# Exp writes runs of 32 tokens, the token order is restored by a permutation matrix in the transpose of x, and all PSUM tiles share four two-bank slots

## Chip, cores, metric

One core of one Trainium2 chip. The metric is the device time of one execution in microseconds (us). In the profile, PE is the engine of matmuls, PEld its weight loads, ACT the scalar engine, DVE the vector engine, POOL the GpSimd engine that issues the casting loads, SP the engine that issues stores.

## The reference

Attention over keys and values that are averaged over 8 neighbouring tokens, then a gated feed-forward block with a convolution of width 3 along the tokens:

```python
# batch 8, heads 8, tokens 576, head dim 64; keys and values pooled to 72
scores = scale * q @ mean8(k).T;  attn = softmax(scores);  y = attn @ mean8(v)
x = y.transpose(0, 2, 1, 3).reshape(8, 576, 512)
h = relu(x @ w_in)                       # 512 -> 1024
c = conv_w[0]*h[t-1] + conv_w[1]*h[t] + conv_w[2]*h[t+1]
out = (h * sigmoid(c)) @ w_out           # 1024 -> 512
```

The queries are loaded with the tokens of a head spread over 96 partitions. The softmax division comes after the product with v, through a column of constants beside v.

## The kernel before

It works batch by batch. While the feed-forward of batch b runs in eight blocks `fb` (mm1, relu, conv, tanh, gate), the attention of batch b+1 is woven in; then mm2 writes the output. A scheduler orders the instructions of each engine at build time, from its own estimate; every engine then executes its list in that fixed order. Cuts are marked with `# ...`.

```python
big_psum = tile_pool(name="big_psum", bufs=3, PSUM)   # two banks each: scores, mm1, conv
one_psum = tile_pool(name="one_psum", bufs=2, PSUM)   # one bank each: all else
q_view = "h (p c) d -> p h c d"          # partition p holds tokens 6p .. 6p+5, 1536 bytes in a row
# ...
def scores(b, h):
    ps = big_psum.tile([P, 2, 512], FP32, name="sc_ps", tag="big")
    for c2 in range(2):                  # two matmuls: tokens of even and of odd c
        nc.tensor.matmul(out=ps[0:Sp, c2, 0:SC], lhsT=kz[b % 2][:, h, c2, :], rhs=qT[:, h % 2, :], ...)
    at = attnT_pool.tile([Sp, S], BF16, name="attnT")
    nc.scalar.activation(                # writes into token order: a step of 6 bf16 = 12 bytes
        out=at.rearrange("s (p cp c2) -> s c2 cp p", cp=QC // 2, c2=2),
        in_=ps[0:Sp, :, 0:SC].rearrange("s c2 (cp p) -> s c2 cp p", cp=QC // 2),
        func=ACT.Exp, scale=1.0 / (POOL * 8.0))
def av(b, i, g):                         # tile i of 128 tokens, four heads: one bank
    ps = one_psum.tile([P, 4, D + 1], FP32, name="av_ps", tag="one")
    # ... four matmuls, one reciprocal of 4 columns, one product into x (256 columns)
def xt(b, i):                            # four transposes of one token tile, one copy to xT
    ps = one_psum.tile([P, n_pairs, P], BF16, name="xt_ps", tag="one")
    # ...
def mm2(b, j):                           # one output tile: one bank, eight matmuls
    ps = one_psum.tile([P, d_model], FP32, name="o_ps", tag="one")
    # ...
```

The softmax here doesn't subtract the row's maximum and nothing guards it: scores larger than these inputs give would overflow.

## Time and profile before

357.72 us, median of two runs (357.71 and 357.73); the profiled execution spans 355.1 us.

| what | value |
|---|---|
| first feed-forward matmul starts at | 40.5 us |
| fifth and sixth batch together (198.5 to 279.0 us) | 80.5 us, 40.25 each |
| from the first to the last exp of such a batch | 18.7 us |
| ACT busy in a middle batch | 26.0 us, of that exps 16.1 |
| PE busy in a middle batch | 31.3 us |

A batch is counted here from its first mm1 matmul to that of the next. The page's line of busy times, with its share of the span, and the chain that ended last:

```profile
PE 264.0 (74%) x2049; PEld 169.0 (48%) x2049; DVE 176.3 (50%) x497; ACT 210.4 (59%) x209; POOL 26.4 (7%) x55
...
ACT 40%; PE 37%; DVE 14%; issue 5%; DMA 3%; ACTq 0%
ACT attnT L182 32%; PE o_ps L277 17%; PE h_ps L238 9%; PE c_ps L257 7%; ACT tg L265 4%; DVE x L206 4%; DMA v_126<-in_v_dram 3%; ACT hT L245 3%; PE av_ps L195 2%; DVE gT L271 2%; DVE o L288 2%; PE xt_ps L219 1%; DVE xT L221 1%; DVE r L205 1%; PE q_ps L152 1%
```

No engine is busy throughout, but a third of the span hangs on one line, the exp. The groups of instructions show why (line, engine, operation, output and input, count; then busy us, the mean of one in ns, idle time before them and what ended it):

```profile
L182 ACT ACTIVATE attnT<-sc_ps 72x576 bf16<-72x576 f32 x64 | 128.0, 2216 | 13.4 <-PE sc_ps L165 13.4
...
L245 ACT ACTIVATE hT<-h_ps 128x576 bf16<-128x576 f32 x64 | 48.1, 754 | 36.9 <-PE h_ps L238 36.9
L265 ACT ACTIVATE tg<-c_ps 128x576 bf16<-128x576 f32 x64 | 41.9, 654 | 8.4 <-PE c_ps L257 4.7 <-DVE tg_2126 L269 0.4 <-DVE tg_1219 L269 0.4
L206 DVE TENSOR_TENSOR x<-av_ps,r 128x256 bf16<-128x256 f32 x80 | 33.5, 419 | 0.8
```

Exp, relu and tanh each work on 576 columns. The exp takes 2.2 us where the others take 0.65 to 0.75. The table of stretches, two of one batch and two whole batches (stretch and its length, then busy time and count by engine, granted PE clock, DMA share, GB/s):

```profile
93.20:112.20 19.00, 11.63 (x95) 7.94 (x94) 6.17 (x16) 19.00 (x16) 0.79 (x1) 1.00 0.53 93
112.20:130.60 18.40, 16.74 (x131) 9.72 (x130) 11.87 (x36) 5.05 (x9) 0.17 (x2) 1.00 0.13 48
198.50:238.90 40.40, 31.46 (x264) 20.12 (x261) 18.15 (x55) 26.00 (x26) 0.94 (x3) 1.00 0.20 48
238.90:279.00 40.10, 31.23 (x255) 20.41 (x254) 16.37 (x52) 25.96 (x26) 0.17 (x2) 0.96 0.07 27
```

The first line is the exp stretch: ACT (the fifth number) is busy for all 19.00 us. In the second line PE (the second number) is busy for 16.74 of 18.40.

PE's waits on DVE, from the list of waits (us in total, times, longest):

```profile
PE av_ps L195 <- DVE x L206: 4.7, 8, 0.7
PE xt_ps L219 <- DVE x L206: 4.2, 9, 0.8
PE o_ps L277 <- DVE o L288: 4.1, 7, 0.7
```

### The profile page before, as it was taken

The numbers are of one execution on the slowest core, as the hardware profiler recorded it, in microseconds if no ns is written. First come the engines' busy times: TensorE is split into PE (matmuls) and PEld (weight loads), VectorE is DVE, ScalarE is ACT, GpSimd is POOL, SyncE is SP. The second block draws the span as 40 slices with busy tenths as digits, with TensorE's granted clock in tenths as the row PEclk, the third lists the DMA queues.
The fourth block names the chain that finished last, engine by engine and source line by source line (L and its number), as shares of the span: only waits on it lengthen the run. The fifth ranks groups of instructions, "written<-read, shape, count | busy, mean of one in ns | idle before, by whom it ended". The sixth has DMA issues, their size and how long they took to land.

```text
span 355.1 us, 5143 instructions
## 1 busy us (share of the span) xinstructions
PE 264.0 (74%) x2049; PEld 169.0 (48%) x2049; DVE 176.3 (50%) x497; ACT 210.4 (59%) x209; POOL 26.4 (7%) x55
## 2 busy tenths in 40 slices
PE   0163686789867896688777896689757898689995
PEld 0141464454545554464545554464635555454752
DVE  4672875696624934275425742283414732273341
ACT  1097049940798229960898139950996239960751
POOL 7250102112000000000000000000000000000000
PEclk9999999898999999899989999999998998999999
DMA  7999992969950030401140030501100030001103
GB/s 178 228 197 204 167 168 32 178 87 131 242 77 8 0 150 0 68 0 61 59 66 3 23 127 0 69 0 65 55 0 2 3 147 0 2 0 61 59 20 130
DMA packets 26957, 27.23 MB, mean 77 GB/s; under 512 B 3869, under 2 KB 21173, under 8 KB 26933
## 3 DMA queue, kind: packets, MB, share of 16 engines
q0 software_dynamic: 20464, 15.09, 30.0%
q1 hardware_dynamic: 5844, 10.63, 8.4%
q10 hardware_dynamic: 624, 1.18, 1.3%
q8 instruction: 16, 0.26, 0.3%
q14 instruction: 9, 0.07, 0.1%
HBM read 32.52 MB, written 9.44 MB: 118 GB/s over the span
## 4 chain that ended last, share of the span: by engine, by line
ACT 40%; PE 37%; DVE 14%; issue 5%; DMA 3%; ACTq 0%
ACT attnT L182 32%; PE o_ps L277 17%; PE h_ps L238 9%; PE c_ps L257 7%; ACT tg L265 4%; DVE x L206 4%; DMA v_126<-in_v_dram 3%; ACT hT L245 3%; PE av_ps L195 2%; DVE gT L271 2%; DVE o L288 2%; PE xt_ps L219 1%; DVE xT L221 1%; DVE r L205 1%; PE q_ps L152 1%
## 5 line engine op out<-in xcount | busy, mean ns | idle before, releaser
L182 ACT ACTIVATE attnT<-sc_ps 72x576 bf16<-72x576 f32 x64 | 128.0, 2216 | 13.4 <-PE sc_ps L165 13.4
L238 PE MATMUL h_ps<-xT,w_in_sb 128*128 128x288 bf16 x512 | 84.6, 304 | 2.0 <-DVE xT L221 0.5
L257 PE MATMUL c_ps<-hT,dw 128*128 128x288 bf16 x384 | 62.5, 295 | 20.3 <-ACT attnT L182 19.9
L245 ACT ACTIVATE hT<-h_ps 128x576 bf16<-128x576 f32 x64 | 48.1, 754 | 36.9 <-PE h_ps L238 36.9
L277 PE MATMUL o_ps<-w_out_sb,gT 128*128 128x512 bf16 x288 | 65.6, 382 | 5.7 <-DVE o L288 4.1
L238 PEld LDWEIGHTS <-w_in_sb 128*128 128x128 bf16 x512 | 49.6, 102 | 19.5 <-issue 5.9
L286 ACT COPY o<-o_ps 128x512 f32<-128x512 f32 x16 | 9.4, 586 | 77.9 <-PE o_ps L277 77.9
L257 PEld LDWEIGHTS <-dw 128*128 128x128 bf16 x384 | 37.6, 101 | 35.7 <-issue 25.5
L265 ACT ACTIVATE tg<-c_ps 128x576 bf16<-128x576 f32 x64 | 41.9, 654 | 8.4 <-PE c_ps L257 4.7
L277 PEld LDWEIGHTS <-gT 128*128 128x128 bf16 x288 | 27.6, 98 | 39.1 <-issue 6.0
L288 DVE COPY o<-o_ps 128x512 f32<-128x512 f32 x20 | 13.8, 691 | 44.2 <-PE o_ps L277 44.2
L206 DVE TENSOR_TENSOR x<-av_ps,r 128x256 bf16<-128x256 f32 x80 | 33.5, 419 | 0.8
L195 PEld LDWEIGHTS <-attnT 72*128 72x128 bf16 x320 | 18.8, 104 | 27.2 <-ACT attnT L182 13.4
L158 DVE COPY qT<-q_ps 128x576 bf16<-128x576 bf16 x32 | 14.6, 457 | 31.4 <-PE q_ps L152 31.0
L205 DVE RECIPROCAL r<-av_ps 128x4 f32<-128x4 f32 x80 | 13.8, 177 | 25.1 <-PE av_ps L195 24.4
L165 PE MATMUL sc_ps<-qT,kz_107 128*72 128x288 bf16 x64 | 14.3, 325 | 14.4 <-ACT attnT L182 8.5
L195 PE MATMUL av_ps<-va_109,attnT 72*128 72x65 bf16 x160 | 13.8, 208 | 11.8 <-ACT attnT L182 8.0
L165 PE MATMUL sc_ps<-qT,kz_108 128*72 128x288 bf16 x64 | 13.4, 304 | 10.6 <-ACT attnT L182 9.7
L219 PE MATMUL xt_ps<-ident,x 128*128 128x128 bf16 x160 | 18.0, 234 | 4.2 <-DVE x L206 4.2
L221 DVE COPY xT<-xt_ps 128x512 bf16<-128x512 bf16 (+1 forms) x40 | 15.7, 392 | 2.9 <-PE xt_ps L219 2.9
L219 PEld LDWEIGHTS <-x 128*128 128x128 bf16 x160 | 11.3, 102 | 11.5 <-DVE x L206 8.5
L195 PE MATMUL av_ps<-va_110,attnT 72*128 72x65 bf16 x160 | 12.1, 199 | 6.0 <-ACT attnT L182 3.1
(231 smaller groups left out, 186.8 us busy)
## 6 DMA issues: line engine op xcount, KB each, us to landing
out_dram<-o SPq DMA_DIRECT2D x36, 256.0 KB
kr<-in_k_dram POOLq DMA_DIRECT2D x7, 576.0 KB, 13.5
qr<-in_q_dram POOLq DMA_DIRECT2D x7, 576.0 KB, 6.4
vr<-in_v_dram POOLq DMA_DIRECT2D x7, 576.0 KB, 13.1
w_in_sb<-in_moe_w_in_dram POOLq DMA_DIRECT2D x4, 256.0 KB, 14.2
w_out_sb<-in_moe_w_out_dram POOLq DMA_DIRECT2D x2, 512.0 KB, 12.6
v_112<-in_v_dram ACTq DMA_DIRECT2D x2, 288.0 KB
k_111<-in_k_dram SPq DMA_DIRECT2D x2, 288.0 KB
```

Source lines behind the costliest of these rows:

```text
L165: nc.tensor.matmul(out=ps[0:Sp, c2, 0:SC], lhsT=kz[b % 2][:, h, c2, :], rhs=qT[:, h % 2, :], start=True, stop=True,)
L182: nc.scalar.activation(out=at.rearrange("s (p cp c2) -> s c2 cp p", cp=QC // 2, c2=2), in_=ps[0:Sp, :, 0:SC].rearrange("s c2 (cp p) -> s c ...
L195: nc.tensor.matmul(out=ps[:, hh, :], lhsT=st[b]["at"][h][:, t0:t0 + P], rhs=va[b % 2][:, h, :], start=True, stop=True,)
L206: nc.vector.tensor_tensor(out=st[b]["x"][i][:, 4 * g:4 * g + 4, :], in0=ps[:, :, 0:D], in1=r.unsqueeze(2).to_broadcast([P, 4, D]), op=OP.mult,
L219: nc.tensor.transpose(out=ps[:, pr, :], in_=x[:, 2 * pr:2 * pr + 2, :], identity=ident)
L221: nc.vector.tensor_copy(out=st[b]["xT"][:, :, i * P:tok0[i] + P], in_=ps[:, :, new:P])
L238: nc.tensor.matmul(out=ps[:, c, 0:SC], lhsT=w_in_sb[:, dc, fb * P:(fb + 1) * P], rhs=xT[:, dc, c * SC:(c + 1) * SC], start=(dc == 0), stop ...
L245: nc.scalar.activation(out=hT[:, fb, 1:S + 1].rearrange("p (c n) -> p c n", c=NS), in_=ps[:, :, 0:SC], func=ACT.Relu, scale=0.5,)
L257: nc.tensor.matmul(out=ps[:, c, 0:SC], lhsT=dw[:, fb, kk, :], rhs=hT[:, fb, c * SC + kk:c * SC + kk + SC], start=(kk == 0), stop=(kk == KW ...
L265: nc.scalar.activation(out=tg.rearrange("p (c n) -> p c n", c=NS), in_=ps[:, :, 0:SC], func=ACT.Tanh)
L277: nc.tensor.matmul(out=ps, lhsT=gT[:, fb, j * P:(j + 1) * P], rhs=w_out_sb[:, fb, :], start=(fb == 0), stop=(fb == n_fb - 1),)
L288: nc.vector.tensor_copy(out=o, in_=ps)
```

## The change

Its intent is to make the exp's writes nearly contiguous. q is loaded as pairs of neighbouring tokens, so that one score matmul makes the even tokens and the other the odd ones. The exp then writes runs of 32 even and 32 odd tokens; within each 64 tokens the order is off, and a permutation matrix, put in place of the identity in the transpose of x, restores it. All PSUM tiles come from one ring of four two-bank slots, and evictions are merged: q by four heads, av by eight heads, xT by two token tiles, mm2 by two output tiles per slot. Two columns of zero pad on each side of h, instead of one, put it on an even start. The core of the diff (cuts marked):

```diff
-    QC = S // QP
+    QC = S // (2 * QP)
+    GRP = 32
-    big_psum = ctx.enter_context(tc.tile_pool(name="big_psum", bufs=3, ...))
-    one_psum = ctx.enter_context(tc.tile_pool(name="one_psum", bufs=2, ...))
+    psum = ctx.enter_context(tc.tile_pool(name="psum", bufs=4, ...))
+    def slot(name):
+        return psum.tile([P, 2, BANK], FP32, name=name, tag="slot")
-    q_view = "h (p c) d -> p h c d"
+    q_view = "h (c p two) d -> p h c (two d)"      # runs of 512 bytes
# ...
         nc.scalar.activation(
-            out=at.rearrange("s (p cp c2) -> s c2 cp p", cp=QC // 2, c2=2),
-            in_=ps[0:Sp, :, 0:SC].rearrange("s c2 (cp p) -> s c2 cp p", cp=QC // 2),
+            out=at.rearrange("s (m two j) -> s two m j", two=2, j=GRP),
+            in_=ps[0:Sp, :, 0:SC].rearrange("s two (m j) -> s two m j", j=GRP),
# ...
-    def av(b, i, g):
-        ps = one_psum.tile([P, 4, D + 1], FP32, name="av_ps", tag="one")
+    def av(b, i):                                  # all eight heads, one reciprocal, one product
+        ps = slot("av_ps")
# ...
-            nc.tensor.transpose(out=ps[:, pr, :], in_=x[...], identity=ident)
+            nc.tensor.transpose(out=y[:, pr, ii * P:(ii + 1) * P], in_=..., identity=perm)
# ...
+    def build_perm():
+        for g in range(P // (2 * GRP)):
+            for two in range(2):
+                r0 = g * 2 * GRP + two * GRP
+                nc.vector.tensor_copy(
+                    out=perm.rearrange("p (g j two) -> p g two j", two=2, j=GRP)[:, g, two, :],
+                    in_=ident[:, r0:r0 + GRP])
# ... qT, xT and mm2 merged in the same way; x_pool 4 -> 5, qT_pool 6 -> 4, o_pool four one-tile buffers -> two two-tile ones
# ... the places where q, av and xt of the next batch are woven in are shifted to fit
```

## The prediction

> **What bounds the kernel now.** The chain of waits of the 355.1 us span is ACT 40%, PE 37%, DVE 14%; the exp (attnT<-sc_ps) alone holds 32%. By the table of stretches, a middle batch takes about 40 us in two regimes:
> - The exp stretch (93.2 to 112.2 us, four blocks with two exps each): ACT busy 19.00 of 19.00 us, exps 15.94 of that, PE only 11.63. PE waits for exps (list of waits: c_ps 19.9 us, sc_ps 18.2 us).
> - The rest (112.2 to 130.6): PE busy 16.7 of 18.4, PE bound.
> The last batch, without exps, is PE bound (12.69 of 13.00). The first feed-forward matmul comes at 40.5 us (timeline), after eight exps in a row (17.4 to 32.9) that start when loads have landed.
>
> **Why the exp is slow.** It writes 576 columns in about 2.0 us (groups: 128.0 us for 64). Tanh, same columns, contiguous output, takes 0.65. The exp's output steps 12 bytes. The Trainium skill, "SBUF — State Buffer", section Door 1: The DMA port swizzle, says consecutive accesses within one 16-byte line run at full bandwidth and a crossing pays; "ScalarE: Activation LUTs", section What ACT_TABLE_LOAD costs, gives 186 ns + 0.833 ns per column = 0.67 us, which the tanh agrees with. Runs of 32 bf16 are 64 bytes, so I expect 0.67 to 0.72 us (estimate).
>
> **Removed.** About 1.35 us of ACT per exp, 85 us in all, useful only down to PE's level. Exp stretch: ACT need falls to 4 x (0.66+0.66+2x0.68) = 10.7 us, PE needs 11.6 plus gaps; 19.0 becomes about 12: 7 us x 7 batches = 49 us. Prologue: the exps become load bound, saving about 7 us.
> DVE: reciprocals and x multiplies merge (80 to 40 each: 177+419 ns twice becomes about 185+690), qT copies 32 to 16, xT 40 to 24: about 16 us less DVE, mostly off the chain, 2 us on it. gT and relu gain little from the even pad.
>
> **Added.** (a) q loads in 512-byte reads instead of 1536: about 14,000 more packets. Now 20,464 software packets take 30% of 16 engines, 83 ns each at 737 bytes; small ones perhaps 45 ns (estimate): 40 us per engine over the run, harmless in the middle, but the first 55 us run at 0.9 DMA share: +1 to 4 us there. (b) One ring of four two-bank slots: a slow DVE eviction now blocks mm1 and conv too: +0.5 to 1 us per batch, +3 to 7 us. (c) The permutation is a moving matrix of the same size and type, so free; building it is eight small DVE copies. PE's count of work is unchanged.
>
> **Sum.** 357.7 - 49 - 7 - 2 - 3 (existing gaps closed) + 2 + 4 = about 303; from below (prologue 33, batches of 31 us PE work plus 1 to 2 us gaps, last 26, 2.6 outside the span) 295. Middle: 299 us, range 287 to 314. Faster by over 2%: 0.96, within 2%: 0.03, slower: 0.01.
>
> **What would show each step.** Exp mean 0.6 to 0.75 us, ACT busy about 120. Exp below 6% of the chain, PE above 65%. A middle batch of 32 to 34 us, exp stretch about 12. First mm1 at 31 to 35 us. PE busy 85 to 90%. DVE busy 155 to 165 us. Software packets about 34,000. PE waiting on DVE evictions (x, qT, xT) more than now.
>
> **What would make it wrong.** Short runs still costly on ACT (exp 1.2 us: about 320). The shared ring serialising PE behind DVE (10 to 20 us). q loads landing late in batches 0 to 1. An order that sets evictions behind trees. A lower granted clock under denser PE work.

## More of the kernel before

The timeline inside an exp stretch (start, duration, engine and line; in brackets the idle time before and what ended it):

```profile
107.78 4.03 ACT L182 ACTIVATE attnT<-sc_ps 72x576 bf16<-72x576 f32 x2
107.96 1.14 PE L238 MATMUL h_ps<-xT,w_in_sb 128*128 128x288 bf16 x8
109.94 0.90 PE L257 MATMUL c_ps<-hT,dw 128*128 128x288 bf16 x6 [0.84 <-ACT attnT L182]
110.68 0.19 PE L195 MATMUL av_ps<-va_109,attnT 72*128 72x65 bf16 x1
111.39 0.90 ACT L245 ACTIVATE hT<-h_ps 128x576 bf16<-128x576 f32 x1
```

PE waits for a PSUM slot that an exp holds. The relu behind the exp takes 0.90 us, but its record begins before that of the exps ends (107.78 + 4.03 = 111.81), so it adds only 0.48 us behind them. Note also how PE's busy time is made: six conv matmuls standing alone count 0.90 us, one single av matmul counts 0.19.

## The result

274.92 us, median of two runs (273.04 and 276.79); the ratio to before is 0.7685, with a 95% interval of 0.746 to 0.791. A later timing (run a0_after_again) gave 274.73 us (0.7689, interval 0.7641 to 0.7737). The direction was forecast. The size was not: the fastest time in the forecast range was 287.

The profile after, its busy times and chain (span 271.3 us):

```profile
PE 235.3 (87%) x2049; PEld 165.5 (61%) x2049; DVE 165.7 (61%) x391; ACT 125.3 (46%) x209; POOL 29.7 (11%) x55
...
PE 66%; DMA 21%; issue 6%; DVE 4%; POOL 1%; ACT 1%; POOLq 0%; DVEq 0%
PE o_ps L291 20%; PE h_ps L246 19%; PE c_ps L266 15%; DMA qr<-in_q_dram 7%; DMA kr<-in_k_dram 5%; DMA w_in_sb<-in_moe_w_in_dram 5%; DMA vr<-in_v_dram 4%; PE sc_ps L174 4%; PE av_ps L195 3%; PE xt_ps L222 3%; PE q_ps L161 2%; POOL qr L96 1%; DVE o L301 0%; PE kT_ps L134 0%; DVE t_2519 L114 0%
```

The exp has left the chain. The same groups:

```profile
L253 ACT ACTIVATE hT<-h_ps 128x576 bf16<-128x576 f32 x64 | 41.6, 651 | 42.7 <-PE h_ps L246 42.7
...
L182 ACT ACTIVATE attnT<-sc_ps 72x576 bf16<-72x576 f32 x64 | 37.6, 640 | 26.4 <-PE sc_ps L174 26.4
...
L206 DVE TENSOR_TENSOR x<-av_ps,r 128x512 bf16<-128x512 f32 x40 | 27.3, 687 | 0.6
```

The exp fell to 0.640 us. Two product instructions of x at 419 ns became one of 687. The relu's record fell by 0.10 us as well. Two of PE's waits on DVE in the list before, those for x, shrank, the third, for o, is gone, and one for q grew:

```profile
PE sc_ps L174 <- DVE qT L165: 11.6, 7, 4.7
...
PE xt_ps L222 <- DVE x L206: 1.9, 2, 1.3
...
PE av_ps L195 <- DVE x L206: 0.5, 1, 0.5
```

The stretches: the first two batches, the exps of a middle batch, and the fifth and sixth batch:

```profile
32.90:70.30 37.40, 30.51 (x246) 20.86 (x245) 28.05 (x55) 14.94 (x25) 6.37 (x10) 0.95 1.62 161
70.30:107.20 36.90, 32.04 (x269) 21.75 (x268) 24.22 (x47) 16.51 (x28) 4.33 (x7) 0.95 0.95 145
137.90:146.20 8.30, 8.30 (x78) 6.85 (x77) 4.01 (x10) 7.95 (x15) 1.19 (x1) 1.00 0.65 62
162.20:187.00 24.80, 24.80 (x245) 18.67 (x244) 15.45 (x37) 14.35 (x25) 1.33 (x3) 1.00 0.34 57
187.00:217.20 30.20, 30.20 (x270) 21.02 (x269) 15.27 (x36) 16.18 (x28) 0.15 (x2) 1.00 0.14 53
```

In the fifth and sixth batch PE is busy for all 55.00 us: 27.5 us a batch, where the prediction's floor of PE work was 31. The first two batches are different, at 37 us each.

Where the 83.8 us of span went: start of the first feed-forward 40.5 to 32.9 (7.6 less), first two batches 78.6 to 74.3 (4.3 less), third to seventh batch 200.2 to 134.8 (65.4 less), the rest 35.8 to 29.3 (6.5 less).

How a batch can take less time than PE was "busy" before is seen in the chain, where the pieces of a row of matmuls count only from one start to the next:

```profile
115.79 0.49 PE sc_ps L174 x4
116.28 0.98 PE h_ps L246 x8
117.26 0.74 PE c_ps L266 x6
...
120.21 0.52 PE av_ps L195 x16
```

Six conv matmuls cost 0.74 us in a row, not 0.90, and sixteen av matmuls 0.52, not sixteen times 0.19. The steps from start to start inside groups, median, are 122 ns for mm1 and scores, 123 for conv, 216 for mm2, 56 for the transposes of x, 43 for those of q, 33 for av, 32 for those of k, and they are the same in both traces to 1 ns. Times their counts in a batch (64 mm1, 48 conv, 36 mm2, 16 scores, 24 q, 40 av, 20 x, 8 k) they make 27.2 us. So the trace of before already held the right floor. PE's busy time there, 31.3 us, held another 4.1 us: tails of short groups that end in a wait, and some matmuls at a lower clock (granted clock 0.96 in one of the two batches).

The Trainium skill says as much: "Trainium Kernel Development and Optimization", section Performance Expectations, calls matmul busy time a bad metric for how close a kernel is to its roofline, because matmuls are pipelined. "TensorE: Matmul & The Clock Gate", section "Wait — 56ns, not 53.3ns?", gives columns divided by 2.4 GHz plus about 2.5 ns for a full-clock step. An estimate worked out from it is 122.5, 215.8 and 55.8 ns for 288, 512 and 128 columns; this trace agrees, with 122, 216 and 56.

### The profile page after: what moved, and what is told of

Same layout as the page of the kernel before. It is cut to its first block, busy times and chain, and to the rows that moved or that the text cites. A ratio compares the mean times of both kernels' runs of the same rounds, so it can differ in the third digit from the quotient of the medians.

```text
span 271.3 us, 5046 instructions
## 1 busy us (share of the span) xinstructions
PE 235.3 (87%) x2049; PEld 165.5 (61%) x2049; DVE 165.7 (61%) x391; ACT 125.3 (46%) x209; POOL 29.7 (11%) x55
## 3 DMA queue, kind: packets, MB, share of 16 engines
q0 software_dynamic: 32752, 15.09, 51.9%
## 4 chain that ended last, share of the span: by engine, by line
PE 66%; DMA 21%; issue 6%; DVE 4%; POOL 1%; ACT 1%; POOLq 0%; DVEq 0%
PE o_ps L291 20%; PE h_ps L246 19%; PE c_ps L266 15%; DMA qr<-in_q_dram 7%; DMA kr<-in_k_dram 5%; DMA w_in_sb<-in_moe_w_in_dram 5%; DMA vr<-in_v_dram 4%; PE sc_ps L174 4%; PE av_ps L195 3%; PE xt_ps L222 3%; PE q_ps L161 2%; POOL qr L96 1%; DVE o L301 0%; PE kT_ps L134 0%; DVE t_2519 L114 0%
## 5 line engine op out<-in xcount | busy, mean ns | idle before, releaser
L246 PE MATMUL h_ps<-xT,w_in_sb 128*128 128x288 bf16 x512 | 77.5, 296 | 0.3 <-ACT tg L274 0.3
L253 ACT ACTIVATE hT<-h_ps 128x576 bf16<-128x576 f32 x64 | 41.6, 651 | 42.7 <-PE h_ps L246 42.7
L182 ACT ACTIVATE attnT<-sc_ps 72x576 bf16<-72x576 f32 x64 | 37.6, 640 | 26.4 <-PE sc_ps L174 26.4
L206 DVE TENSOR_TENSOR x<-av_ps,r 128x512 bf16<-128x512 f32 x40 | 27.3, 687 | 0.6
L161 PE MATMUL q_ps<-ident,qr 96*128 96x96 bf16 x192 | 12.6, 219 | 8.4 <-DMA qr<-in_q_dram 8.1
L222 PE MATMUL xt_ps<-perm,x 128*128 128x128 bf16 x160 | 14.5, 231 | 2.0 <-DVE x L206 1.9
L161 PEld LDWEIGHTS <-qr 96*128 96x128 bf16 x192 | 10.7, 105 | 9.0 <-DMA qr<-in_q_dram 8.4
L195 PEld LDWEIGHTS <-attnT 72*128 72x128 bf16 x320 | 14.2, 102 | 1.9 <-DVE x L206 0.6
L107 POOL DMA_DIRECT2D qr<-in_q_dram x7 | 8.3, 1189 | 61.8 <-PE sc_ps L174 57.8
L174 PE MATMUL sc_ps<-qT,kz_106 128*72 128x288 bf16 x64 | 11.6, 295 | 3.3 <-DVE qT L165 3.3
L174 PEld LDWEIGHTS <-kz_105 128*72 128x72 bf16 x64 | 7.7, 130 | 10.6 <-DVE qT L165 8.5
L165 DVE COPY qT<-q_ps 128x1152 bf16<-128x1152 bf16 (+1 forms) x18 | 12.4, 688 | 1.5 <-PE q_ps L161 1.1
## 6 DMA issues: line engine op xcount, KB each, us to landing
w_out_sb<-in_moe_w_out_dram POOLq DMA_DIRECT2D x2, 512.0 KB, 10.7
```

The source lines that it names most:

```text
L161: nc.tensor.transpose(out=ps[:, i // 2, o0:o0 + QP], in_=src[:, h0 + i, c, :], identity=ident[0:QP, 0:QP])
L182: nc.scalar.activation(out=at.rearrange("s (m two j) -> s two m j", two=2, j=GRP), in_=ps[0:Sp, :, 0:SC].rearrange("s two (m j) -> s two m ...
L195: nc.tensor.matmul(out=ps[:, h // 4, c:c + D + 1], lhsT=st[b]["at"][h][:, t0:t0 + P], rhs=va[b % 2][:, h, :], start=True, stop=True,)
L206: nc.vector.tensor_tensor(out=x.rearrange("p (g h) d -> p g h d", g=2), in0=y[:, :, :, 0:D], in1=r.unsqueeze(3).to_broadcast([P, 2, 4, D]) ...
L222: nc.tensor.transpose(out=y[:, pr, ii * P:(ii + 1) * P], in_=st[b]["x"][i][:, 2 * pr:2 * pr + 2, :].rearrange("p h d -> p (h d)"), identit ...
L246: nc.tensor.matmul(out=ps[:, c, 0:SC], lhsT=w_in_sb[:, dc, fb * P:(fb + 1) * P], rhs=xT[:, dc, c * SC:(c + 1) * SC], start=(dc == 0), stop ...
```

## The experiments

Two questions. Which part of the change made the gain that the prediction lacked: theory D says the exp alone (PE's need was over-read), its rival R says the shared ring and the merged evictions. And why are the first two batches slow: packets of the short q reads (P), or the fixed order of the vector engine (O)?

A warning on results. Worked out on a computer with the reference for one batch, giving the queries the wrong token order changes the output by 0.5% in norm, because q and k are drawn so small that the attention weights are nearly equal. So a pass says little about token order here; the right order of the right kernels rests on reading their code.

In the table, "batch" is half the time of the fifth and sixth batch together in the profiled run, and "first two" the sum of the first two. Ratios are to the kernel before, in the same rounds.

| run | edit | us | ratio | batch | first two |
|---|---|---|---|---|---|
| before | | 356.4 | 1 | 40.25 | 78.6 |
| x1 | before, exp contiguous | 290.4 | 0.814 | 30.55 | 62.7 |
| x2 | before, q layout, runs of 32, permutation | 292.2 | 0.819 | 30.5 | 63.5 |
| y1 | x2 in one ring | 288.1 | 0.807 | 29.6 | 77.7 |
| y2 | y1 with av merged | 280.2 | 0.785 | 28.35 | 65.8 |
| changed, again | none | 274.7 | 0.769 | 27.5 | 74.0 |
| x3 | changed, exp step 12 bytes | 344.6 | 0.965 | 39.2 | 80.7 |
| x6 | changed, exp step 4 bytes, no permutation | 275.2 | 0.772 | 27.85 | 75.2 |
| x4 | changed, long q reads | 269.2 | 0.754 | 27.5 | 70.6 |
| x5 | changed, trees pinned | 272.3 | 0.765 | 30.25 | 60.9 |
| z2 | x5, k's pin four blocks earlier, three output buffers | 264.6 | 0.741 | 28.1 | 64.1 |
| z1 | z2 with long q reads | 266.5 | 0.748 | 28.55 | 62.0 |

Three cautions. First, y2, z1, z2 and z3 ran on chip 0, the other experiments on chip 4; the kernel before took 356.9 us on the one and 356.4 to 356.5 on the other. Second, compare "first two" only among kernels with the same pools. By the steps above, the matmuls that start in the first two batches need 46 us in before, x1 and x2, but 54 in the kernels with the ring, whose order does mm2 work there that the others do in the last batch (29 to 30 us of need in the last batch against 22 to 24). Third, an edit can change the scheduler's order. Compared record by record, PE, DVE and ACT run the same order in x1 as in before, and in x3 and x4 as in the changed kernel; x2 adds four copies on DVE; y1 and y2 have orders of their own.

### The changed kernel again

> The changed kernel, unedited, as the yardstick on this chip: 272 to 277 us. Middle batches (third to seventh feed-forward start) 27.5 us on average, the first two about 37 us each. No theory is tested by it; it says how far two chips differ.

274.73 us; middle batches as before, the first two 39.4 and 34.6 us. The sum of the two varies little (74.0 against 74.3), so this is a yardstick.

### x1: the exp alone

```diff
-                out=at.rearrange("s (p cp c2) -> s c2 cp p", cp=QC // 2, c2=2),
-                in_=ps[0:Sp, :, 0:SC].rearrange("s c2 (cp p) -> s c2 cp p", cp=QC // 2),
+                out=at.rearrange("s (c2 n) -> s c2 n", c2=2),
+                in_=ps[0:Sp, :, 0:SC],
```

> The kernel before with one edit: exp writes its 576 columns contiguously (token order wrong, so the result is wrong on purpose). Theory D (my sum failed because I took PE's busy time, which holds the tail of every short group, for PE's need; at the steps seen inside full groups a middle batch needs only 27.2 us of PE): the exp alone frees it, middle batches 28 to 30 us, total 275 to 288 us. Theory R (the shared ring and the merged evictions carry the gain beyond my 49 us): exp alone gives what I had summed for it, 295 to 305 us. In both the exp's mean falls to 0.6 to 0.7 us. If the relu's mean falls from 0.754 to 0.65 us here, without the even pad, the exp in front of it had lengthened it.

290.41 us, between the two theories' ranges. Its groups, then the stretch of exps of a middle batch and the fifth and sixth batch:

```profile
L245 ACT ACTIVATE hT<-h_ps 128x576 bf16<-128x576 f32 x64 | 41.7, 654 | 45.8 <-PE h_ps L238 45.6
...
L182 ACT ACTIVATE attnT<-sc_ps 72x576 bf16<-72x576 f32 x64 | 37.6, 640 | 18.0 <-PE sc_ps L165 18.0
```

```profile
175.50:184.50 9.00, 8.95 (x82) 6.95 (x80) 4.31 (x13) 8.28 (x15) 0.84 (x1) 1.00 0.24 26
161.10:192.50 31.40, 29.73 (x262) 20.08 (x262) 18.12 (x55) 15.90 (x26) 1.01 (x3) 1.00 0.26 62
192.50:222.20 29.70, 28.06 (x256) 19.45 (x257) 16.45 (x52) 15.86 (x26) 0.17 (x2) 1.00 0.10 36
```

The exp stretch falls from 18.7 to 9.0 us, not to 12: that is D's part, 9.7 us a batch instead of 7. The rest of a batch stays as it was, 21.5 us both times (40.25 less 18.7, 30.55 less 9.0). So the exp alone takes the batch to 30.55 us, and the 3 us that still lie between it and 27.5 belong to something else in the change. Both theories are half right. The relu fell to 654 ns here, without the even pad, and x3 puts it back to 753: the 12-byte writes in front of it lengthened its record, not the odd start.

### x2: layout, runs and permutation with the old pools

The diff is the layout, runs and permutation parts of the change; pools, evictions and pad stay.

> The kernel before with q's layout, runs of 32 and the permutation (a right result), but its own PSUM pools (three two-bank, two one-bank slots), unmerged evictions and odd pad. Theory D: 276 to 290 us, that is within 5% of the changed kernel; theory R: 295 us or more. The difference to the changed kernel is the worth of ring, merging and pad; the difference to x1 is the worth of q's shorter reads and the new token order.

292.19 us, again between the ranges. The new layout with its short reads and permutation costs 1.8 us against x1, hardly more than the runs of one kernel scatter. Pools, merging and pad are worth 17.5 us (292.2 less 274.7), where the prediction had summed about 1 us for them (2 and 3 gained, 4 lost).

### y1 and y2: ring, then merged av

```diff
-    big_psum = ... bufs=3 ...; one_psum = ... bufs=2 ...
+    psum = ctx.enter_context(tc.tile_pool(name="psum", bufs=4, ...))     # y1: all tiles tag="slot"
```

> The run with old pools (292 us) with one edit: all its PSUM tiles in one ring of four two-bank slots, evictions still unmerged (q by head pairs, x by four heads, xT and out by single tiles). Theory ring: the middle batch falls from 30.5 us to 28.5 or less, total 275 to 283, since four slots are open to any stage where only two one-bank slots served q, av, xT and out. Theory merging: it is the halved number of evictions and round trips that pays, the middle batch stays at 29.5 to 31 us, total 286 to 295.

288.12 us. A middle batch fell by 0.9 us, to 29.6. It is in the range of the theory "merging". The new pools come with a new order, so the 0.9 us is the worth of both together. The run's first batch took 47 us under the order that the scheduler made for it, so its total is worth less than its middle batches.

y2 gives `av` one slot and one pair of DVE instructions for all eight heads, as in the changed kernel.

> The ring with unmerged evictions (288.1 us, middle batch 29.65 us) with one edit: av fills one two-bank slot for all eight heads, so one reciprocal and one x product per token tile instead of two. If the halved round trips of av are what the merging pays with: the middle batch falls to 28.2 us or less, total 274 to 281. If q's, xT's and out's merging matter as much: about 29, total 282 to 287. Unclear if the first batch's time moves by more than that (it was 47 us in the run this one edits, 40 in others).

280.18 us, batch 28.35: 1.25 us less than y1. The total is in the first forecast's range, the batch 0.15 above it; what is left to 27.5, 0.85 us, is the merging of q, xT and out with the new places and buffer counts that go with it, and the pad, which were not separated. So the 3.0 us fall to ring 0.9, av merging 1.25 and the rest 0.85. The idle time that PE spends in the fifth and sixth batch together, summed from the records, goes the same way: 17.8 us before, 3.3 in x2 (it waits for DVE to finish x and out), 2.6 in y1 (now it waits for ACT's tanh), 0.8 in y2 and none in the changed kernel. From x2 on that is half of the gain, 1.65 us a batch; the other half is shorter busy time of PE (28.9 us a batch in x1, 27.5 in the changed kernel).

### x3: the exp alone undone

```diff
-            out=at.rearrange("s (m two j) -> s two m j", two=2, j=GRP),
-            in_=ps[0:Sp, :, 0:SC].rearrange("s two (m j) -> s two m j", j=GRP),
+            out=at.rearrange("s (p cp two) -> s two cp p", cp=QC, two=2),
+            in_=ps[0:Sp, :, 0:SC].rearrange("s two (cp p) -> s two cp p", cp=QC),
```

> The changed kernel with the exp alone undone: it writes with a step of 12 bytes again (token order wrong, so the result is wrong on purpose; the order of instructions on PE and DVE is the same as in the changed kernel). If exp and ring act independently: 356 minus 17 = 339, range 333 to 345 us, exp mean 2.0 to 2.3 us. If the ring only pays once the exp is out of the way: 350 to 358. Relu mean back to 0.75 us if the exp in front lengthens it.

344.59 us, just inside the range for independent parts; exp mean 2.216, relu 0.753:

```profile
L253 ACT ACTIVATE hT<-h_ps 128x576 bf16<-128x576 f32 x64 | 48.1, 753 | 41.0 <-PE h_ps L246 41.0
```

The parts are not independent. With a slow exp, ring and merging gain 1 us a batch (40.25 to 39.2); with a fast one 3. The exp is worth 66.0 us on the old pools and 69.9 on the ring.

### x6 and z3: how the exp's time depends on its step

```diff
-    GRP = 32
+    GRP = 1        # x6; and identity=ident, build_perm() left out
```

> The changed kernel with runs of one token instead of 32: the exp writes with a step of 4 bytes straight into token order, so no permutation is needed and the result is right. Theory L (what counts is how many neighbouring writes fall in one 16-byte line: four here, 1.33 at a step of 12): exp mean 0.62 to 0.70 us, total 271 to 277. Theory S (any step over one element is slow): exp mean above 1.2 us, total above 295. In between would be a cost per byte of step.

```profile
L182 ACT ACTIVATE attnT<-sc_ps 72x576 bf16<-72x576 f32 x64 | 47.2, 811 | 20.5 <-PE sc_ps L174 20.5
```

The exp took 0.811 us, in neither range: not free, and not slow. The total, 275.20 us, equals the changed kernel's within 0.2%, as theory L had it. With runs of one token there is nothing to permute, so permutation matrix and runs of 32 could be left out at no loss that shows in the total (a middle batch grew by 0.35 us): what mattered is q's load by token pairs, which turns a step of 12 bytes into one of 4.

> A probe, wrong on purpose: in each batch head 0's exp writes contiguously, heads 1 to 6 with a step of 2, 3, 4, 6, 8 and 16 elements (4, 6, 8, 12, 16, 32 bytes), head 7 in runs of four. Known: step 1 0.64 us, runs of 32 0.64, step 2 0.81, step 6 2.2. Theory L (a cost for each 16-byte line entered): time rises with the step up to 8 elements and is flat beyond, step 3 about 1.0, step 4 about 1.3, steps 8 and 16 2.5 or more and equal; runs of four (8 bytes, then a jump of 16) between 0.64 and 1.3. Theory T (a threshold): up to some step the cost of step 2, beyond it the cost of step 6, nothing between.

L183 is head 0 (contiguous), L185 to L195 are steps of 4, 6, 8, 12, 16 and 32 bytes, L197 is runs of four:

```profile
L193 ACT ACTIVATE attnT<-sc_ps 72x576 bf16<-72x576 f32 x8 | 23.7, 2959 | 0.0
L195 ACT ACTIVATE attnT<-sc_ps 72x576 bf16<-72x576 f32 x8 | 21.7, 2717 | 0.0
L191 ACT ACTIVATE attnT<-sc_ps 72x576 bf16<-72x576 f32 x8 | 16.9, 2114 | 3.2 <-PE sc_ps L174 3.2
L189 ACT ACTIVATE attnT<-sc_ps 72x576 bf16<-72x576 f32 x8 | 12.0, 1506 | 0.0
L187 ACT ACTIVATE attnT<-sc_ps 72x576 bf16<-72x576 f32 x8 | 9.2, 1147 | 2.9 <-PE sc_ps L174 2.9
L197 ACT ACTIVATE attnT<-sc_ps 72x576 bf16<-72x576 f32 x8 | 8.1, 1006 | 0.0
L185 ACT ACTIVATE attnT<-sc_ps 72x576 bf16<-72x576 f32 x8 | 6.5, 809 | 0.0
L183 ACT ACTIVATE attnT<-sc_ps 72x576 bf16<-72x576 f32 x8 | 5.1, 638 | 12.5 <-PE sc_ps L174 12.5
```

The mean rises steadily with the step: 0.81, 1.15, 1.51, 2.11 and 2.96 us for 4, 6, 8, 12 and 16 bytes, then 2.72 for 32. Two of these means depend on what runs in front. The exp of 16 bytes always follows that of 12 bytes at once, and its record begins about 0.4 us before the other's ends; the exp of 32 bytes follows a tanh in seven of eight cases (about 2.69 us) and the exp of 16 bytes in one (2.94). So 16 and 32 bytes cost about the same. 576 elements at 4, 6, 8 and 12 bytes enter 144, 216, 288 and 432 lines of 16 bytes, at 16 and 32 bytes 576. From 144 lines (0.81) to 576 (2.72) the exp grows by 4.4 ns for each line more, and 6, 8 and 12 bytes lie within 0.07 us of that straight line. Theory L's shape, a cost for each line entered, fits, though its figures for 6 and 8 bytes were too low; theory T falls. The runs of four settle nothing: they too enter 144 lines and took 1.01 us, not 0.81, but they always follow the exp of 32 bytes, with records that overlap by about 0.5 us.

### x4: longer q reads

```diff
-    q_view = "h (c p two) d -> p h c (two d)"
+    q_view = "h (p c two) d -> p h c (two d)"
```

> The changed kernel with one edit in q's load: each partition takes six neighbouring tokens, so reads are of 1536 bytes instead of 512 (tokens land in another order, result wrong on purpose; the order of instructions on PE and DVE is the same). Theory P (the first two batches, 37 us each against 27.5 later, are slow because 14,000 more packets delay the loads): they fall to 30 to 33 us and the total to 262 to 268. Theory O (they are slow because the vector engine's fixed order puts k and v trees of batches far ahead in front of work that is due, and waits there for their loads): the trees wait nearly as long as before, total 268 to 275. Software packets back to about 20,500.

269.20 us: 5.5 less than the changed kernel, in O's range and not in P's. The first batch fell from 39.4 to 33.6 us, the second rose from 34.6 to 37.0; neither came to P's 30 to 33. So P holds for part of the first batch only. In the profiled runs the first two batches gained 3.4 us of the 5.5. The short reads cost 5.5 us here, against about 2 in the prediction.

### x5: trees pinned

The chain after has its DMA part before 84 us. What happens there is seen in the timeline of the changed kernel:

```profile
83.52 1.22 DVE L114 TENSOR_TENSOR t_2519<-kr 72x2048 bf16<-72x2048 bf16 x1 [1.93 <-DMA kr<-in_k_dram]
...
84.88 0.75 DVE L165 COPY qT<-q_ps 128x1152 bf16<-128x1152 bf16 x1
...
85.68 1.18 PE L174 MATMUL sc_ps<-qT,kz_105 128*72 128x288 bf16 x4 [4.69 <-DVE qT L165]
```

PE waits 4.69 us for a copy of q; DVE has it next in its list, but first stands the sum of keys of batch 6, while batch 1 runs (counted from 0), and its load has not landed. The edit keeps the sums behind the last gate product traced before them (order only, on the one engine):

```diff
+        with tc.issue_after(st["gate"]) if "gate" in st else nullcontext():
             k_tree(b, st[b]["k"], 0, H)        # and the same for v_tree
# ... st["gate"] is set to each gate product
```

> The changed kernel, right result, with k's and v's trees of the next batch kept in the vector engine's order behind the last gate product traced before them (order only, no added wait); in the changed kernel they stand up to five batches ahead. Theory O (this order makes the first two batches slow): they fall from 37 us each to 28 to 32, total 256 to 266 us. Theory P (only the loads' bandwidth does): no more than 3 us gained, total 270 to 275. Middle batches stay at 27.5 us in both.

The first two batches fell to 29.1 and 31.8 us, as O forecast; the total, 272.29 us, did not, and O's forecast that the middle batches stay at 27.5 us failed. The gain was given back in the batches after: 30.25 us instead of 27.5. Where, the timeline of this run shows:

```profile
88.77 0.80 POOL L105 DMA_DIRECT2D kr<-in_k_dram  x1 [1.32 <-DVE t L114]
89.10 11.79 SPq L304 DMA_DIRECT2D out_dram<-o  x5
...
99.84 0.69 DVE L303 COPY o<-o_ps 128x512 f32<-128x512 f32 x1 [8.85 <-DMA out_dram<-o]
100.58 2.08 PE L248 MATMUL h_ps<-xT,w_in_sb 128*128 128x288 bf16 x8 [4.76 <-DVE o L303]
```

With the sums in step, the load of k for a later batch is freed just when the output is stored; the store is late, the two output buffers run out, and PE stands 4.76 us. In the changed kernel all loads of k and v were issued by 82 us, and later stores met none but q's.

### z2 and z1: pins elsewhere, a third output buffer, then long q reads

The edit against x5:

```diff
-        with tc.issue_after(st["gate"]) if "gate" in st else nullcontext():
+        with tc.issue_after(st["gates"][b - 2, 3]) if b > 1 else nullcontext():    # z2, for k
-    o_pool = ctx.enter_context(tc.tile_pool(name="o", bufs=2))
+    o_pool = ctx.enter_context(tc.tile_pool(name="o", bufs=3))                      # z2
```

> The changed kernel with trees pinned as in the pinned run (272.3 us), but k's behind the gate product of block 3 of two batches earlier, so that the load it frees runs in mid batch and not beside the output stores, and three output buffers instead of two. In the pinned run the first two batches were 29.1 and 31.8 us but the next four lost 2 to 4 us each in one wait for an output buffer (a store took 8.0 us beside a k load). If that collision was the cause: all of batches two to seven at 25 and 30 us, total 259 to 265. If the wait stays: 268 to 272.

264.63 us (ratio 0.741), in the range at its upper end, and the fastest version here. PE has no wait for an output buffer left in the batches looked at; a middle batch is 28.1 us, 0.6 over the changed kernel's, and part of that is waiting for x (0.3 to 0.7 us in each batch). That sums of k now stand before av's evictions is the likely reason, not shown by a run. Place of the pin and third buffer were not separated.

z1 adds the reads of 1536 bytes with the token order restored in DVE's copy of q:

```diff
+                out=qT[:, 2 * j:2 * j + 2, :].rearrange("d h (p c) -> d h p c", c=QC),
+                in_=ps[:, j, 0:2 * SC].rearrange("d (h c p) -> d h p c", h=2, c=QC),
```

> The run with pins and three output buffers plus q in reads of 1536 bytes, the token order restored by a strided eviction of q on the vector engine, so the result is right. The long reads gained 5.5 us without pins, 3.4 of it in the first batch's start; with pins perhaps 2 to 4. The vector engine takes about 0.4 us more per q eviction, beside its load of 62%. Expected 3 us below the run with pins and buffers: 256 to 262; if the strided eviction stalls scores, equal or slower than that run.

266.47 us, 1.8 more than z2: a miss of the range, though the forecast named the case. Scores wait 6.8 us in all for q's copy, against 3.1 in z2. The strided copy of q costs DVE 23.5 us in all, against 12.4 for the merged plain one, and the middle batch grew by 0.45 us.

## Why the prediction was right or wrong

| term of the sum | predicted | measured |
|---|---|---|
| exp, in the batches | -49 | -62.6 (x1 less before, -66.0, without the start's -3.4) |
| start, by the exp | -7 | -3.4 (40.5 to 37.1 us in x1) |
| merged evictions, gaps, ring | -2 -3 +4 | -17.5 (changed less x2) |
| short q reads | +2 | 5.5 (changed less x4); with the new order 1.8 on the old pools (x2 less x1, hardly clear of the scatter) |
| total | -55 to -63 | -81.7 (changed again less before) |

Right:
- That ACT bound the exp stretch ("the rest" was bound by PE only in part, see below), the exp's new time (0.6 to 0.75 in the list of checks, 0.640 measured, a little under the estimate of 0.67 to 0.72), ACT busy about 120 (125.3), DVE busy 155 to 165 (165.7, just outside), software packets about 34,000 (32,752).
- The first mm1 at 31 to 35 us (32.9), but partly by luck: in x1 the exp moved it by 3.4 us and not by 7, and the other parts of the change gave the rest.
- The exp below 6% of the chain (it is not in it), PE above 65% there (66%), PE busy 85 to 90% (87%). The named risk of a lower granted clock did not come: 0.966 to 0.976 before, 0.981 to 0.987 in the changed kernel, in the same rounds.

Missed besides the total: a middle batch of 32 to 34 us (27.5), an exp stretch of about 12 us (8.3), and PE waiting more on DVE's evictions, which came about for q alone.

Wrong, two steps:
1. "PE needs 11.6 plus gaps; 19.0 becomes about 12". 11.63 was PE's busy time in that stretch. The matmuls that started in it (34 mm1, 24 conv, 12 scores, 12 q, 12 av) need 9.5 us at the steps above. x1 shows the stretch at 9.0 us from first to last exp, so the term was 2.7 us a batch too small. ACT's need beside it, "10.7 us", was too high as well: in x1's stretch ACT is busy for 8.28 us with 15 instructions, since the records of neighbours overlap. The same reading made the count from below, "batches of 31 us PE work", too high: the need is 27.2, and the changed kernel's batches take 27.5.
2. "One ring of four two-bank slots: ... +0.5 to 1 us per batch" and the merging "mostly off the chain, 2 us on it". The sign was wrong. Outside the exp stretch PE did wait, for DVE to empty the two one-bank slots; a busy share of 16.74 in 18.40 hid it, since the tails counted as work: by the steps above, the matmuls that started there need 15.7. Ring and merging, with the orders that came with them, took 3 us out of each middle batch: 0.9, 1.25 and 0.85 by the series x2, y1, y2, changed kernel. In the profiled runs the third to seventh batch make 18.8 us of the difference (153.6 in x2, 134.8 changed).

"q loads landing late in batches 0 to 1" was named as a risk, and it came about: 5.5 us instead of 2. But it is only part of why those batches take 74 us; the vector engine's order is another (x5). Of the gain that the prediction did not see, 13.6 us is the first step (62.6 less 49) and 16.5 the second (17.5 less 1), less the 3.6 that the start fell short in x1.

What stays open: how much of ring and merging is slots and how much is the scheduler's new order, which of q, xT, out and pad makes the last 0.85 us of a batch, and whether z2's pin or its third buffer removed the wait for stores.

## What to carry to other kernels

PE's busy time is no measure of PE's need where matmuls come in short groups between waits: take the start-to-start steps inside full groups, times the counts, and use that as the floor. A strided write can set the speed of an ACT instruction: shorten the step in the layout of the load before adding a permutation (here a step of 4 bytes made an exp of 0.81 us, runs of 64 bytes one of 0.64, and the totals were the same, because PE set the pace). Once a bound is removed, look at the batches that did not reach the new floor: here a fixed instruction order ran sums up to five batches ahead of their loads.

## What the Trainium skill lacked or had wrong

- "SBUF — State Buffer", section Door 1: The DMA port swizzle, says that full bandwidth needs at least two accesses in a 16-byte line and that one can stride for free up to 8 bf16. For ACT writes it isn't free: the 576-column exp took 0.81 us at a step of 2 bf16, 1.15 at 3, 1.51 at 4, 2.11 at 6 and 2.96 at 8, against 0.64 contiguous; about 4.4 ns for each line entered, and no more beyond 16 bytes (2.72 at 32). The line of 16 bytes itself agrees with these runs.
- "ScalarE: Activation LUTs", section What ACT_TABLE_LOAD costs, gives 186 ns + 0.833 ns per column (666 ns for 576) and an overlap of about 93 ns back to back. The records are 640 to 655 ns, and a contiguous exp takes 588 ns of ACT (37.6 us for 64), so it agrees within 4%; that the record of an instruction behind a strided write is lengthened (relu 753 ns on average instead of 651 to 654) and overlaps the one in front is on no page that I read.
- "TensorE: Matmul & The Clock Gate", section Back-to-back issue gap, gives about 81 ns a matmul at 128 columns and 131 at 512 for streams of weight load and matmul, and keeps the step by columns for a matmul alone. Here each matmul has its own weight load, and inside full groups the steps are 56 and 216 ns, those by columns. With 96 columns (q) the runs show 43 ns and with 65 (av) 33 ns, so loads of 128 weight columns were hidden in steps as short as 33 ns.
